# Merging attention runs on TensorE, and a first half turned ahead of the first scores, in a hash attention kernel with an MLP behind it

## The chip, the cores and the metric

One core of one Trainium2 chip. The metric is device time of one execution in microseconds (us), as a median over the runs of a kernel. Executions of one kernel mostly agree within 0.3%; where a single microsecond is at stake, four or five runs on the same chip are compared. All runs here count as fast runs, but for one outlier of the kernel before that is named at e1. Times inside a trace are counted from the start of the profiled execution, whose span is about 2 us shorter than the time of that run.

Below, "PE" is TensorE's matmul, "PEld" its weight load, "DVE" VectorE, "ACT" ScalarE, "POOL" GpSimd. A "bank" is an accumulator of 128 x 512 fp32 in PSUM that TensorE writes into; the kernel has eight of them in use. "Start to start" is the time from the start of one group of instructions to the start of the next; it is what a group costs on a busy engine, where the printed duration contains the overlap with its neighbour.

## The reference, cut to what matters

```python
# hash attention: 4 batches, 8 heads, 768 positions, 64 wide; proj is 64 x 6
q_bits = (q @ proj) > 0;  k_bits = (k @ proj) > 0          # six bits, a bucket each
mask   = bucket(q)[:, None] == bucket(k)[None, :]
scores = where(mask, q @ k.T / 8, -1e9)
attn   = exp(scores - max) ; attn /= sum(attn) + 1e-9
x      = (attn @ v)                     # heads side by side: 3072 tokens x 512
# MLP: 512 -> 2048 -> 512
h = x @ w_in
g = maximum(h, 0) + alpha * minimum(h, 0)
out = g @ w_out
```

The kernel works on 16 pairs of heads. For each pair it transposes q and k ("turn"), multiplies them by proj and takes the signs ("hash"), and then does two units of 384 queries each: 32 units in all. In a unit, six key blocks of scores go through the exponential, "attend" multiplies the probabilities by v, and "totals" multiplies their sums by a matrix of ones to get the divisor. The mask is folded into the scores as a bf16 product of the sign bits. After attention comes the MLP as seven-product blocks (a Strassen-like scheme on 2 x 2 pieces): 44 blocks, each with three accumulators a, b and c.

## The kernel before

Helpers (cut; `do` issues an instruction, `psum` is the pool of banks):

```python
def turn(pi, name, half):                       # three transposes into one bank, one copy
    ps = psum.tile([P, CW], F32, ..., tag="mi")
    for i in range(CH):
        do(PE.transpose(ps[:, i * P : (i + 1) * P], src[:, CH * half + i], ident))
    do(ACT.activation(tr[name, pi][:, half...], ps, AF.Copy, ...))

def hash_bits(pi, half):                        # four products, three signs
    ps = psum.tile([P, CW], F32, ..., tag="mi")
    ...

def scores(u, part):                            # two key blocks
    for kc in (2 * part, 2 * part + 1):
        sc = psum.tile([P, 2, 512], F32, ..., tag="sc")      # a double bank; two of them
        for what, first in ((bits, True), (tr, False)):
            for s in range(2):
                do(PE.matmul(sc[:, s, :CW], what["k", pi]..., what["q", pi]..., start=first, stop=not first))
        do(ACT.activation(pt[:, :, :CW], sc[:, :, :CW], AF.Exp, ...))

def magnitude(pi, name):                        # square in place; its maximum is for the verdict
    do(ACT.activation(t, t, AF.Square, accum_out=mags[...]))
```

One unit of the main loop, cut to what occupies TensorE and to the loads:

```python
for u in range(UNITS):
    pi, g = divmod(u, NCH)
    scores(u, 0)
    ...
    if more:                                    # a next pair exists
        if g == 0: turn(pi + 1, "q", 0); turn(pi + 1, "q", 1)
        else:      hash_bits(pi + 1, 0)
    if u > 0: attend(u - 1, 0)
    scores(u, 1)
    ...
    if u > 0: attend(u - 1, 1); totals(u - 1)
    scores(u, 2)
    if u > 0: divide(u - 1)
    if more:
        if g == 0: turn(pi + 1, "k", 0); turn(pi + 1, "k", 1)
        else:      hash_bits(pi + 1, 1)
    ...
    if more:
        magnitude(pi + 1, "qk"[g])
        if pi + 2 < NPAIR: load(pi + 2, "qk"[g])
```

The eight banks: "sc" two double banks, "mi" two, "av" two. A product of the MLP takes its a from "sc", its b from "mi", its c from "av", so each of them has two buffers. A gate of the MLP (`g`) is written by VectorE into memory that the attention's tiles held before:

```python
attn.close()                                    # attention's tiles are free
late.append(ctx.enter_context(tc.tile_pool(name="late", bufs=2)))
...
g_m[m, i] = late[0].tile([P, CW], F32, ...)
do(DVE.scalar_tensor_tensor(g_m[m, i], h, al, h, op0=ALU.mult, op1=ALU.max))
```

In the third block a verdict is worked out (are the inputs in the range for which the fast path is right): three reductions on VectorE, then four times a transpose on TensorE and a maximum on VectorE.

## Time and profile before

| | us |
|---|---|
| time, median of 3 runs | 976.89 |
| span of the profiled execution | 973.3 |
| first transpose on TensorE | 6.11 |
| first score | 12.73 |
| first attend | 24.43 |
| end of the last totals of attention | 386.00 |
| start of f_3a, just after the verdict | 412.40 |

The table is read as three stages: a head up to the first attend, in which TensorE often waits; 362 us of attention, in which it is seen waiting only once, for 0.25 us; and the MLP, in which it is busy too. The view of all waits confirms that TensorE's idle time was small and mostly at the head; the largest wait elsewhere is the verdict's, 2.0 us. Its columns are: engine and line, then what it waited for; after the colon the total, the number of waits and the longest.

```profile
PE tp_q L629 <- DMA qn<-in_q_dram: 6.1, 1, 6.1
PE sc L668 <- ACT pt L673: 2.6, 2, 2.4
PE vd L861 <- DVE top L856: 2.0, 1, 2.0
```

So 6.1 us go before any input is there, and most of the 2.6 us is one wait at 19.40 us. No change to waits alone could win much in the middle.

### The profile page before, as it was taken

To read this page: it belongs to the slowest core of one execution; us is meant where nothing else is said; L and a number is where in the kernel's file an instruction comes from. 1 tells how busy PE (TensorE), PEld (TensorE's weight loads), DVE (VectorE), ACT (ScalarE), POOL (GpSimd) and SP (SyncE) were. 2 spreads that over 40 slices of the span, in tenths; PEclk is the share of its full clock that TensorE was granted. 3 is DMA by queue.
4 is the path that set the end of the run, shared out by engine and by line. 5 is a ranking of instruction groups with operands and counts; after the bars stand their busy time and mean duration, and the time that the engine had idled before them with its cause. 6 is when DMAs were issued, how large, how long until landed. Compare 5 with 4: busy or idle time off the path is not lost.

```text
span 973.3 us, 12433 instructions
## 1 busy us (share of the span) xinstructions
PE 953.9 (98%) x4741; PEld 589.9 (61%) x4741; DVE 552.9 (57%) x995; ACT 371.5 (38%) x669; POOL 64.8 (7%) x62
## 2 busy tenths in 40 slices
PE   6999999999999999999999999999999999999997
PEld 3444444444444444556888556888556888556885
DVE  3788888898998887765400665301666301666000
ACT  6777776777777773222000222001222001222000
POOL 1000110000000010000300000200001200000000
PEclk9999999999999999999999999999999999999999
DMA  8767879699777643844100234100234100221000
GB/s 208 166 157 174 217 175 291 164 224 225 193 198 193 161 125 88 347 190 140 49 23 33 76 113 143 47 24 31 76 114 154 47 22 22 87 103 38 22 22 25
DMA packets 102020, 119.40 MB, mean 123 GB/s; under 512 B 53808, under 2 KB 88640, under 8 KB 101952
## 3 DMA queue, kind: packets, MB, share of 16 engines
q1 hardware_dynamic: 91680, 105.54, 34.7%
q0 software_dynamic: 8704, 12.58, 7.6%
q8 instruction: 39, 0.64, 0.3%
q10 hardware_dynamic: 1568, 0.39, 0.2%
q14 instruction: 29, 0.24, 0.1%
HBM read 78.65 MB, written 27.26 MB: 109 GB/s over the span
## 4 chain that ended last, share of the span: by engine, by line
PE 97%; ACT 1%; DVE 1%; DMA 0%; issue 0%; SPq 0%; ACTq 0%; DVEq 0%
PE sc L668 16%; PE av L703 14%; PE z_2a L773 6%; PE z_1a L773 6%; PE z_0a L773 6%; PE z_2c L773 3%; PE z_1c L773 3%; PE z_0c L773 3%; PE hs L651 2%; PE f_0a L773 2%; PE sm L715 2%; PE f_2a L773 2%; PE f_3a L773 2%; PE f_7a L773 2%; PE f_6a L773 2%; PE f_5a L773 2%
## 5 line engine op out<-in xcount | busy, mean ns | idle before, releaser
L673 ACT ACTIVATE pt<-sc 128x768 f32<-128x768 f32 x192 | 150.3, 813 | 97.4 <-PE sc L668 92.6
L668 PE MATMUL sc<-qT,kT 64*128 64x384 f32 x768 | 155.2, 482 | 0.0
L703 PE MATMUL av<-pt,vn 128*64 128x385 f32 (+1 forms) x768 | 138.1, 495 | 0.0
L703 PEld LDWEIGHTS av<-pt,vn 128*64 128x64 f32 x768 | 49.4, 136 | 76.7 <-issue 76.7
L827 DVE TENSOR_TENSOR g<-g,g 128x384 f32<-128x384 f32 x128 | 84.0, 677 | 2.2
L668 PEld LDWEIGHTS sc<-qT,kT 64*128 64x128 f32 x768 | 68.7, 189 | 21.0 <-issue 20.9
L668 PE MATMUL sc<-qb,kb 64*128 64x384 bf16 x384 | 63.6, 328 | 2.7 <-ACT pt L673 2.6
L685 POOL DMA_DIRECT2D accp<-pt x32 | 38.5, 1204 | 335.0 <-ACT pt L673 161.3
L668 PEld LDWEIGHTS <-kb 64*128 64x128 bf16 x384 | 19.1, 93 | 66.1 <-issue 52.3
L773 PE MATMUL z_2a<-wo,g 128*128 128x256 f32 x256 | 58.0, 379 | 0.5 <-ACT z_2u L780 0.5
L773 PE MATMUL z_0a<-wo,g 128*128 128x256 f32 x256 | 57.9, 379 | 0.0
L773 PE MATMUL z_1a<-wo,g 128*128 128x256 f32 x256 | 57.9, 379 | 0.0
L773 PEld LDWEIGHTS z_2a<-wo,g 128*128 128x128 f32 x256 | 48.6, 190 | 8.1 <-ACT z_2u L780 0.9
L773 PEld LDWEIGHTS z_0a<-wo,g 128*128 128x128 f32 x256 | 48.6, 190 | 7.5
L773 PEld LDWEIGHTS z_1a<-wo,g 128*128 128x128 f32 x256 | 48.6, 190 | 6.6
L820 DVE SCALAR_TENSOR_TENSOR g<-h,alpha 128x384 f32<-128x384 f32 x32 | 20.8, 652 | 50.5 <-ACT h L812 50.5
L749 POOL TENSOR_TENSOR x<-x,x 128x768 f32<-128x768 f32 x12 | 23.9, 2000 | 359.4 <-DMA x<-x_s 358.9
L654 ACT ACTIVATE qb<-hs,hb 32x384 bf16<-32x384 f32 x64 | 36.7, 573 | 2.3 <-PE hs L651 1.1
L690 DVE TENSOR_TENSOR accd<-accd,pt 128x768 f32<-128x768 f32 x32 | 30.7, 959 | 4.1 <-ACT kT L630 1.0
L693 DVE TENSOR_TENSOR accd<-accd,accp 128x768 f32<-128x768 f32 x32 | 30.5, 952 | 3.1 <-DMA accp<-pt 3.1
L689 DVE TENSOR_TENSOR accd<-pt,pt 128x768 f32<-128x768 f32 x32 | 30.4, 949 | 0.5 <-ACT pt L673 0.5
L682 DVE TENSOR_TENSOR accp<-pt,pt 128x768 f32<-128x768 f32 x32 | 30.5, 952 | 0.0
(218 smaller groups left out, 1443.5 us busy)
## 6 DMA issues: line engine op xcount, KB each, us to landing
wi<-w_in_s SPq DMA_DIRECT2D x32, 896.0 KB, 4.6
accp<-pt POOLq DMA_DIRECT2D x32, 384.0 KB, 7.2
raw<-in_moe_w_in_dram SPq DMA_DIRECT2D x16, 512.0 KB, 4.8
raw<-in_moe_w_out_dram SPq DMA_DIRECT2D x16, 512.0 KB, 4.4
w_in_s<-wsi SPq DMA_DIRECT2D x16, 448.0 KB, 6.8
w_out_s<-wso SPq DMA_DIRECT2D x8, 896.0 KB, 7.5
wo<-w_out_s SPq DMA_DIRECT2D x8, 896.0 KB, 8.4
qn<-in_q_dram SPq DMA_DIRECT2D x32, 192.0 KB, 3.7
```

What stands on the lines that cost most here:

```text
L654: do(ACT.activation(bits["q", pi][D * s : D * s + 32, cols], ps[r], AF.Sign, bias=hb[r]))
L668: do(PE.matmul(sc[:, s, :CW], what["k", pi][r, ks], what["q", pi][r, qs], start=first, stop=not first,))
L673: do(ACT.activation(pt[:, :, :CW], sc[:, :, :CW], AF.Exp, scale=SCALE / DOWN))
L682: do(DVE.tensor_tensor(accp[u], p(u, 0), p(u, 1), op=ALU.add))
L685: nc.gpsimd.dma_start(accp[u], p(u, 2), accum_op=ALU.add)
L689: do(DVE.tensor_tensor(accd[u], p(u, 3), p(u, 4), op=ALU.add))
L690: do(DVE.tensor_tensor(accd[u], accd[u], p(u, 5), op=ALU.add))
L693: do(DVE.tensor_tensor(accd[u], accd[u], accp[u], op=ALU.add))
L703: do(PE.matmul(av[u][D * s : D * s + D, :w], nat["v", pi][:, s, kc * D : (kc + 1) * D], prob[u, kc][:, s, :w], start=(kc == 0), stop=(kc = ...
L749: do(engine.tensor_tensor(x_m[b, to], x_m[b, a], x_m[b, c], op=ALU.subtract))
L773: do(PE.matmul(self.ps[bank], self.left(left, k), self.right(right, k), start=start and k == 0, stop=k == self.nk - 1, skip_group_check=no ...
L827: do(DVE.tensor_tensor(g_m[to, i], g_m[x, i], g_m[y, i], op=op))
```

## The change

Its intent is to make TensorE change its kind of work less often, and to start earlier:

1. Score runs of six key blocks (three of this unit and three of the next) in place of three runs of two; the two attend halves and totals side by side; turns of q and k side by side; both hash halves in one group. For this the score banks become three double banks, which turn and hash share; the two banks left, "sm" and "av", become single.
2. The first q and k are loaded in halves, and one half is turned and hashed first; the second half is turned before the first scores too, but hashed behind them.
3. Twelve products of zeros occupy TensorE while the inputs come.
4. The squares (`magnitude`) go behind the exponentials.
5. The verdict's four transposes go into one bank, with one maximum.
6. In the first MLP block the steps are reordered so that c is finished first and b last.

Smaller moves go with these and are not shown below: the order of the first loads, alpha's transpose (now in the second unit), and the places of some of VectorE's additions.

```diff
-    psum = ... tc.tile_pool(name="ps", bufs=2, ...)
+    psum = ... tc.tile_pool(name="ps", bufs=1, ...)
+        zero = const.tile([P, 512], BF16, name="zero")
+        ps = psum.tile([P, 512], F32, name="nil", tag="av")
+        for i in range(12):
+            do(PE.matmul(ps, zero[:, :P], zero, start=True, stop=True))
+    def two_banks(name):
+        return psum.tile([P, 2, 512], F32, name=name, tag="sc", bufs=3)
@@ Product.times
-                tag, shape = {"a": ("sc", ...), "b": ("mi", ...), "c": ("av", ...)}[bank]
+                if bank == "a" or bank == "c" and self.name == "f0_0":
+                    t = two_banks(self.name + bank)[:, 0]
+                else:
+                    t = psum.tile([P, 512], F32, ..., tag="sm" if bank == "b" else "av")
@@ head
-    load(0, "q"); load(0, "k", nc.scalar); setup(); load(0, "v")
-    ... turn(0, name, half) four times, hash_bits(0, half) twice, setup_alpha()
+    load_part(0, "q", slice(0, CH), nc.sync); load_part(0, "k", slice(0, CH), nc.scalar)
+    setup()
+    ... the other halves' loads
+    for name in "qk": turn(0, name, first)
+    hash_bits(0, first)
+    for name in "qk": turn(0, name, second)
+    ... loads of the next pair and of weights
+    scores(0, 0); add_first(0)
+    hash_bits(0, second)
+    for name in "qk": turn(1, name)
@@ main loop, TensorE's work only
-        scores(u, 0) | turn or hash half | attend(u - 1, 0) | scores(u, 1)
-        attend(u - 1, 1), totals(u - 1) | scores(u, 2) | turn or hash half
+        scores(u, 1), scores(u + 1, 0)
+        hash_bits(pi + 1)  or  turn(pi + 2, "q"), turn(pi + 2, "k")
+        attend(u, 0), totals(u), attend(u, 1)
@@ end of the loop body
-            magnitude(pi + 1, "qk"[g]); load(pi + 2, "qk"[g])
+        done = [(u, "q"), (u, "k")] if u < 2 else []
+        if 2 <= pi + 1 + g < NPAIR: done.append((pi + 1 + g, "kq"[g]))
+        for p2, name in done: magnitude(p2, name); load(p2 + 2, name)
@@ first MLP block, verdict
-        for st in ((2, 22, 6, 3, 7) if j == 0 else (2, 22, 5, 6, 3, 7)):
+        for st in ((6, 3, 7, 2, 22) if j == 0 else (2, 22, 5, 6, 3, 7)):
+        ps = psum.tile([1, 4, P], F32, name="vd", tag="av")
         for n in range(4):
-            ... transpose into its own bank, and reduce it
+            do(PE.transpose(ps[:, n], top[:, n : n + 1], ident))
+        do(DVE.tensor_reduce(row, ps, axis=..., op=ALU.max))
```

## The prediction

> **What bounds the kernel now.** I read the page's busy shares first, then the stage table, then the order of work on TensorE inside one unit (384 queries of one pair of heads; there are 32), then the two ends of the attention stage. The metric is 976.89 us; the profiled span is 973.3 us.
>
> ```profile
> PE 953.9 (98%) x4741; PEld 589.9 (61%) x4741; DVE 552.9 (57%) x995; ACT 371.5 (38%) x669; POOL 64.8 (7%) x62
> PE 97%; ACT 1%; DVE 1%; DMA 0%; issue 0%; SPq 0%; ACTq 0%; DVEq 0%
> ...
> 10.00:20.00 10.00, 6.51 (x50) 3.26 (x42) 3.80 (x8) 9.17 (x17) 0.00 (x0) 1.00 0.75 241
> 20.00:40.00 20.00, 20.00 (x140) 8.92 (x137) 15.95 (x28) 16.29 (x29) 2.53 (x2) 1.00 0.76 163
> 200.00:300.00 100.00, 100.00 (x676) 44.28 (x676) 91.55 (x165) 72.12 (x120) 10.80 (x9) 1.00 0.79 201
> 400.00:960.00 560.00, 557.77 (x2168) 411.03 (x2167) 222.41 (x390) 94.41 (x210) 23.89 (x12) 1.00 0.22 78
> ```
>
> Columns of the stage table: stretch, length, then busy us of PE, PEld, DVE, ACT, POOL. TensorE is busy all through the attention stage and the products after it, and the chain that ended last is 97% TensorE. So time can only come from idle TensorE at the head, or from making TensorE's own work shorter. VectorE is second, at 92% in the later attention units. "Busy" says little of how well TensorE is used, so I looked at starts instead of durations:
>
> ```profile
> 104.64 0.88 PE L629 MATMUL tp_q<-ident,qn 128*128 128x128 f32 x6
> 105.45 2.16 PE L703 MATMUL av<-pt,vn 128*64 128x384 f32 x12
> 107.54 0.34 PE L668 MATMUL sc<-qb,kb 64*128 64x384 bf16 x2
> 107.71 0.81 PE L668 MATMUL sc<-qT,kT 64*128 64x384 f32 x4
> 108.35 0.33 PE L668 MATMUL sc<-qb,kb 64*128 64x384 bf16 x2
> 108.52 0.81 PE L668 MATMUL sc<-qT,kT 64*128 64x384 f32 x4
> 109.25 2.16 PE L703 MATMUL av<-pt,vn 128*64 128x384 f32 x12
> 111.24 0.81 PE L715 MATMUL sm<-accd,ones 128*64 128x384 f32 x4
> 111.99 0.34 PE L668 MATMUL sc<-qb,kb 64*128 64x384 bf16 x2
> ```
>
> First column start, second duration. No row waits, yet equal work differs in length. One attend half takes 109.25 to 111.24 = 1.99 us when totals follow in the same tiling (128*64), but 105.45 to 107.54 = 2.09 when scores (64*128) follow. The first score block is 107.54 to 108.35 = 0.81, the second, before another tiling, 0.90. Leaving a tiling therefore costs about 0.09 after scores and 0.10 after attend or totals. Between single records I also find the first attend step 0.05 longer than the later ones (0.37 against 0.32). Hash halves: 0.34 from group to group inside a run, 0.78 for a whole run of two groups, so 0.10 for leaving. A six-transpose run is 0.81, of which 0.15 is beyond 0.11 per transpose.
>
> **What the Trainium skill says.** "TensorEngine Tiling (Array Packing)", Key Properties: "Changing tiling mode (not just tile) drains the TensorE". It gives no time; this trace agrees and puts it at 0.08 to 0.15 us a change. "TensorE: Matmul & The Clock Gate", Part 1: the array starts at half clock and is released after some 3.4 us of sustained work, in a free-running window. The trace agrees: hash groups start 0.64 us apart at 9.05 us and 0.34 apart at 102.14 us. The granted-clock column says 1.00 in both places, so it does not show this. "Perfetto Trace Analysis", Identifying the Most-Contended Engine: matmul busy share is no measure of distance to the limit; here 100% busy hides the drains above.
>
> **The change, part by part.**
>
> Runs merged. Before, a unit on TensorE is seven runs: scores (2 blocks), turn or hash, attend half, scores (2), attend half with totals, scores (2), turn or hash. After, by the order of the built program, it is three: scores (3 of this unit and 3 of the next), turn or hash, attend half + totals + attend half. The arithmetic is the same. Saved per unit: scores leave once in place of three times, 2 x 0.083 = 0.17; attend leaves once in place of twice and refills once, 0.10 + 0.05 = 0.15. Over 31 units: 31 x 0.32 = 9.8 us. Hash halves merged: 14 pairs x 0.107 = 1.5. Turns of q and k merged: 14 pairs x 0.15 = 2.1. In the last two units, 0.36 us of waits for exponentials go with the deeper score buffers (three double banks for two), and the first product's pieces no longer lie between attend pieces, about 0.35. Sum 14.1 us.
>
> Head. Before, first transpose at 6.11, first score at 12.73, first attend at 24.43:
>
> ```profile
> 6.11 1.51 PE L629 MATMUL tp_q<-ident,qn 128*128 128x128 f32 x6 [6.11 <-DMA qn<-in_q_dram]
> ...
> 12.56 0.23 PE L511 MATMUL alps<-ident,alpha 16*128 16x16 f32 x1 [1.13 <-ACT kb L656]
> 12.73 0.34 PE L668 MATMUL sc<-qb,kb 64*128 64x384 bf16 x2
> ...
> 19.40 0.34 PE L668 MATMUL sc<-qb,kb 64*128 64x384 bf16 x2 [2.36 <-ACT pt L673]
> ```
>
> After: twelve zero products of 512 columns start near 1.2 us. From the 0.64 per 2 x 384 columns above, one takes 0.43 cold, so they end near 6.2, no earlier than today's first transpose, though half the input should land near 4.7. What they buy is a full clock. Then three q transposes (0.4), copy (0.57), k copy (0.57), one hash half, three signs of 0.58: first score near 10.7. Three score blocks, hash half two, twelve transposes; then a wait of 0.7 for the second signs and 0.4 for a score bank (ACT, in order, has signs, two copies and the weight's absolute value ahead of the next exponential). First attend near 22.95, with one more score block (0.82) and one more hash half (0.7) done. Gain 1.48 + 0.82 + 0.70 = 3.0 us. The squares (0.84 each plus a read of 0.2), now behind all exponentials, are part of why the 2.36 us wait goes.
>
> Verdict: before, PE waits 1.97 us for VectorE and later 0.26 more between four transposes. The first wait stays (same VectorE work ahead of it), the rest shrinks: 0.45 us.
>
> A new wait. The products' banks b and c go from two buffers to one, and the first product block now finishes c first, b last. The first gate tile lies where attention tiles lay, so its write waits for the last stores:
>
> ```profile
> 387.82 0.62 DVE L730 SCALAR_TENSOR_TENSOR x<-av,vs,dn 128x384 f32<-128x384 f32 x1
> 388.36 1.79 DVE L602 TENSOR_TENSOR wso<-wso 128x256 f32<-128x256 f32 x4
> 390.07 0.55 DVE L815 TENSOR_TENSOR f_0p<-f_0p,f_0b 128x384 f32<-128x384 f32 x1
> 394.25 0.62 DVE L820 SCALAR_TENSOR_TENSOR g<-f_0p,alpha 128x384 f32<-128x384 f32 x1 [3.63 <-issue]
> ```
>
> Today bank b is read at 390.07, before that wait, and the next block has another bank. After, the read of b stands behind the stalled gate write. Let E be the end of the last attend. VectorE then has some 5.4 us left (weight sums, then divide), the store of x lands 2 to 4 us later, so gates begin near E + 8.5 and b is free after four more operations (0.55 + 0.55 + 0.55 + 0.55) at E + 10.7. TensorE wants it after six products of 1.29, at E + 7.7. New wait about 3.0 us.
>
> Sum: 14.1 + 3.0 + 0.45 - 3.0 = 14.6 us; 976.9 - 14.6 = 962.3 us. Everything else (the 560 us of products, the tail) I take as unchanged.
>
> **The rivals.**
>
> 1. VectorE becomes the bound. Its work per unit, start to start, is about 10.4 us in the later units, 11.2 with the x sums of four units. A TensorE unit falls from about 11.57 to 11.14 (4.99 scores + 1.46 turn or hash + 4.68 attend and totals). It still fits; but if VectorE's in-order waits added 0.8 us per unit, half the merge gain (6 us) would go: 968.
> 2. ScalarE holds the longer score runs. A back-to-back exponential takes 0.775 us start to start (1.50 for two) against 0.82 per score block, and there are three double banks. For it: the one four-block run of before stalled 0.3 us with two. If it stalled 0.3 us in every run, 9 us would go: 971. I think the third bank prevents it.
> 3. The new wait does not show, because the stores land sooner: 959.3. Or it is 5 us: 964.3.
> 4. Drains are not saved as counted, since a longer run only hides weight loads that the short one exposed elsewhere: 968 or so. Against it: equal runs differ only by what follows.
>
> **Range and chances.** Independent doubts: head 1.5, merge 2, new wait 2, rivals 1 and 2 one-sided upward. Range 958.0 to 968.0. Over 2% faster means under 957.3, that is 5 us more than I can count: 10%. Slower by 2% would need a stall in every unit well beyond the drains saved: 1%. Within 2%: 89%.
>
> **What would show it.** Right: score blocks 0.82 apart through runs of six, units 11.1 to 11.2 us, first attend near 23 us, end of attention 17 us earlier than its 386 us, and a TensorE gap of some 3 us before f_1b, released by VectorE. Wrong: gaps before scores released by ScalarE, gaps before totals or attend released by VectorE, transposes that still start after 6.5 us cold, or no gap at f_1b.

## The result, and the profile after

The changed kernel took 959.98 us (median of 4 runs, 959.51 to 963.64), beside 976.84 us for the kernel before (4 runs). The ratio is 0.984, with a 95% interval from 0.981 to 0.986: within 2%, and 17 us less. Ratios in this text are the mean time of one kernel's fast runs over that of the other's in the same rounds, so they are not quite the ratio of the medians quoted.

| | before | after |
|---|---|---|
| span of the profiled execution | 973.3 | 957.7 |
| first score | 12.73 | 10.43 |
| first attend | 24.43 | 22.33 |
| end of attention (last totals, or last attend) | 386.00 | 368.22 |
| start of f_1b | 393.85 | 378.60 |
| start of f_3a | 412.40 | 396.75 |

The page's first line and its chain of work that ended last, of the kernel after:

```profile
PE 941.2 (98%) x4753; PEld 600.2 (63%) x4753; DVE 555.2 (58%) x993; ACT 364.7 (38%) x594; POOL 64.6 (7%) x62
...
PE 92%; DVE 4%; ACT 2%; DMA 1%; issue 1%; SPq 0%; DVEq 0%; ACTq 0%
```

TensorE has 12.7 us less busy time for twelve instructions more: the same products became shorter, or overlapped better. But the chain is now only 92% TensorE where it was 97%, although TensorE's time without work fell too, from 19.4 to 16.5 us (span less busy time): at new waits the chain leaves TensorE and runs back along another engine, before 378.60 us along VectorE to about 341 us. So the share says that there are new waits and not what they cost. Both sides have to be found.

**The middle.** The order of work on TensorE in a unit with a turn (columns: start, duration, engine and line, operation and tiles):

```profile
205.71 0.34 PE L695 MATMUL sc<-qb,kb 64*128 64x384 bf16 x2
...
206.53 0.33 PE L695 MATMUL sc<-qb,kb 64*128 64x384 bf16 x2
...
210.66 0.87 PE L646 MATMUL tp_q<-ident,qn 128*128 128x128 f32 x6
211.37 0.82 PE L646 MATMUL tp_k<-ident,kn 128*128 128x128 f32 x6
212.12 2.16 PE L728 MATMUL av<-pt,vn 128*64 128x384 f32 x12
214.11 0.81 PE L740 MATMUL sm<-accd,ones 128*64 128x384 f32 x4
214.75 2.10 PE L728 MATMUL av<-pt,vn 128*64 128x384 f32 x12
216.79 0.34 PE L695 MATMUL sc<-qb,kb 64*128 64x384 bf16 x2
```

Six score blocks take 205.71 to 210.66, 4.95 us. The turns of q and k take 1.46, the first attend half 1.99, totals 0.64, the second attend half, which still leaves its tiling, 2.04. The unit is 216.79 - 205.71 = 11.08 us, where the kernel before needed about 11.57. No row shows a wait.

**The head.** The first transposes, the first scores and the first attend of the kernel after; the bracket names an idle time before the row and what ended it:

```profile
1.20 5.09 PE L509 MATMUL nil<-zero 128*128 128x512 bf16 x12 [1.20 <-DVE wh L501]
6.12 0.49 PE L646 MATMUL tp_q<-ident,qn 128*128 128x128 f32 x3
...
10.43 0.34 PE L695 MATMUL sc<-qb,kb 64*128 64x384 bf16 x2 [1.09 <-ACT kb L675]
...
15.72 0.34 PE L695 MATMUL sc<-qb,kb 64*128 64x384 bf16 x2 [0.45 <-ACT kb L675]
...
22.33 2.16 PE L728 MATMUL av<-pt,vn 128*64 128x385 f32 x12
```

The first transpose starts when the zeros end, at 6.12, and not when its data come; otherwise the head is as wanted, and the first attend is 2.1 us earlier with more work done before it.

**A wait at 32 us**, which nothing in the kernel before corresponds to:

```profile
32.48 0.84 PE L646 MATMUL tp_q<-ident,qn 128*128 128x128 f32 x6 [0.46 <-DMA qn<-in_q_dram]
34.13 0.85 PE L646 MATMUL tp_k<-ident,kn 128*128 128x128 f32 x6 [0.81 <-issue]
```

The turn of the third pair waits for its input. Two input buffers exist, the third pair takes the first pair's, and its load cannot begin before the squares have read that buffer: those are now behind the exponentials, and q's is done at 26.6 us. For k the view names no releaser ("issue"); that it waits for the same reason is shown by e7, where both waits go. From the starts, the two waits cost 0.53 and 0.94 us.

**The end of attention.** TensorE's rows and then VectorE's, of the kernel after:

```profile
374.88 1.45 PE L801 MATMUL f_0a<-x,wi 128*128 128x384 f32 x4
378.60 1.56 PE L801 MATMUL f_1b<-x,wi 128*128 128x384 f32 x4 [2.26 <-DVE f_0p L843]
...
396.31 0.60 PE L889 MATMUL vd<-ident,top 128*1 128x128 f32 x4 [1.97 <-DVE top L884]
```

```profile
376.34 0.62 DVE L848 SCALAR_TENSOR_TENSOR g<-f_0u,alpha 128x384 f32<-128x384 f32 x1 [1.94 <-DMA x_s<-x]
...
378.00 0.55 DVE L843 TENSOR_TENSOR f_0p<-f_0p,f_0b 128x384 f32<-128x384 f32 x1
```

The first gate waits for the store of x, the read of bank b stands three operations behind it at 378.00, and f_1b, which needs the bank, starts 0.6 us later. This is the new wait that the prediction named, with the engine and the product it named: 2.26 us idle, where it said about 3.0. The verdict's wait of 1.97 us stayed, as it said.

**The account.** From the first attend to the end of attention: 361.57 us before, 345.89 after, 15.68 less. Of this, 1.52 is a score block (0.82) and a hash half (0.70) that now come before the first attend, so 14.16 is gain, in spite of about 1.46 lost at 32 us. The head gives 2.10 + 1.52 = 3.6. The new wait, from the starts and not from the idle time alone, takes 2.4 (374.88 to 378.60 is 3.72, against 1.29 for a product). The verdict, from f_2a to f_3a, falls from 4.36 to 3.86, 0.5. Sum 14.2 + 3.6 - 2.4 + 0.5 = 15.9, against 15.6 between the two spans. The medians differ by 16.9: the profiled run of the kernel before, at 975.17 us, was shorter than all four of the runs that its median is of (976.09 to 977.32).

### The profile page after: what moved, and what is told of

Read it like the earlier page. It is cut to its first block, busy times and chain, and to the rows that moved or that the text cites. A ratio compares the mean times of both kernels' runs of the same rounds, so it can differ in the third digit from the quotient of the medians.

```text
span 957.7 us, 12390 instructions
## 1 busy us (share of the span) xinstructions
PE 941.2 (98%) x4753; PEld 600.2 (63%) x4753; DVE 555.2 (58%) x993; ACT 364.7 (38%) x594; POOL 64.6 (7%) x62
## 4 chain that ended last, share of the span: by engine, by line
PE 92%; DVE 4%; ACT 2%; DMA 1%; issue 1%; SPq 0%; DVEq 0%; ACTq 0%
PE sc L695 14%; PE av L728 12%; PE z_2a L801 6%; PE z_1a L801 6%; PE z_0a L801 6%; PE z_2c L801 3%; PE z_1c L801 3%; PE z_0c L801 3%; PE hs L669 2%; PE f_2a L801 2%; PE f_3a L801 2%; PE f_7a L801 2%; PE f_6a L801 2%; PE f_5a L801 2%; PE f_4a L801 2%; PE f_1a L801 2%
## 5 line engine op out<-in xcount | busy, mean ns | idle before, releaser
L700 ACT ACTIVATE pt<-sc 128x768 f32<-128x768 f32 x192 | 152.9, 814 | 78.5 <-PE sc L695 76.6
L728 PEld LDWEIGHTS av<-pt,vn 128*64 128x64 f32 x768 | 52.3, 136 | 70.7 <-issue 61.4
L714 DVE TENSOR_TENSOR accd<-pt,pt 128x768 f32<-128x768 f32 x32 | 30.6, 955 | 14.1 <-ACT pt L700 14.0
L675 ACT ACTIVATE qb<-hs,hb 32x768 bf16<-32x768 f32 (+1 forms) x34 | 29.1, 855 | 10.0 <-PE hs L669 8.7
```

The costliest lines, as they stand in the source:

```text
L675: do(ACT.activation(t[rows].rearrange("p (h w) -> p h w", h=2)[:, halves], ps[ps_rows, halves, :CW], AF.Sign, bias=hb[ps_rows],))
L700: do(ACT.activation(pt[:, :, :CW], sc[:, :, :CW], AF.Exp, scale=SCALE / DOWN))
L714: do(DVE.tensor_tensor(accd[u], p(u, 3), p(u, 4), op=ALU.add))
L728: do(PE.matmul(av[u][D * s : D * s + D, :w], nat["v", pi][:, s, kc * D : (kc + 1) * D], prob[u, kc][:, s, :w], start=(kc == 0), stop=(kc = ...
```

## The experiments

Each edit is made on the changed kernel unless said otherwise. All gave right results. The kernel before had medians of 977.14, 976.92 and 976.17 us on the three chips used (e1 to e4, e5 to e8, e9 to e12).

### e1: the changed kernel again

No edit; a yardstick for e2 to e4.

> The changed kernel unaltered, as the measure for the others, since one of its four runs was 4 us longer than the rest at a granted clock of 0.995. Expected: 959.5 to 960.5 us and a ratio to the kernel before of 0.9825 to 0.9835; the profile as the first one to 0.1 us (first score 10.4 us, first attend 22.3 us, attention over at 368.2 us). If the 964 us comes back in more than one run, then the kernel itself has a second state that one profile does not show.

958.99 us (958.77 to 963.68, 5 runs), ratio 0.982. Its second profile has the first attend at 22.74 and the end of attention at 368.94, so a trace of this kernel repeats to about 0.7 us, not to the 0.1 us expected. One run of the kernel before took 5681.61 us in these rounds, an outlier; the median is not moved by it.

One thing wants an explanation. Of the nine runs of the changed kernel here and above, seven lie at 958.77 to 960.35 with a mean granted clock of 0.998 or 0.999; two lie at 963.64 and 963.68, both at 0.995. The kernel before has such steps too: on the three chips, 10 of its 26 runs (without the outlier) lie at 975.62 to 976.17 with a clock of 0.998 or 0.999, 13 at 976.71 to 977.49 with 0.996 or 0.997, and 3 at 978.26 to 978.90 with 0.995.

### e2: turn or hash between the attend halves

```diff
+        weight_parts(u)
+        attend(u, 0)
         if g == 0 and pi + 1 < NPAIR: hash_bits(pi + 1)
         if g == 1 and pi + 2 < NPAIR: turn(pi + 2, "q"); turn(pi + 2, "k")
-        weight_parts(u)
-        attend(u, 0)
         totals(u)
```

The same instructions, only one more change of tiling in a unit. It tells "a change of kind has a price" from a gain by the deeper score banks or by fewer waits for other engines, which this edit leaves as they are.

> The changed kernel with turn or hash moved from ahead of the attend run to between its two halves: same instructions, but in 28 units one more change of tiling (attend, turn or hash, totals and attend). Theory that each change of tiling costs a drain and a refill: each of the 28 units grows by 0.10 to leave attend and 0.05 to refill it, 0.15 us, so 4.2 us in all; the first attend half goes back from 1.99 to 2.09 us start to start. The rival that the gain came from the deeper score ring or from fewer waits of the other engines: within 0.5 us of the changed kernel, as no wait is added.

963.96 us (963.51 to 964.30, 4 runs), 5.0 above e1. TensorE's rows of its profile, a hash and then a turn inside the attend run:

```profile
205.31 0.87 PE L740 MATMUL sm<-accd,ones 128*64 128x384 f32 x4
206.01 2.11 PE L728 MATMUL av<-pt,vn 128*64 128x385 f32 x12
...
213.00 2.15 PE L728 MATMUL av<-pt,vn 128*64 128x384 f32 x12
215.08 0.87 PE L646 MATMUL tp_q<-ident,qn 128*128 128x128 f32 x6
```

An attend half followed by turn or hash takes 2.09 in place of the 1.99 before totals, and totals 0.70 in place of 0.65. That is 0.15 a unit, and over 29 units with a turn or hash 4.4 us. With a score wait at 30 us (0.5), 0.1 elsewhere and the input wait at 32 us, which went (-1.5), the rows add up to 3.5; the spans of the two profiles differ by 3.9. The price of a change of tiling is real, and the trace shows it as a longer row with nothing waiting.

What the price consists of, this run does not say. In the kernel before, the weight loads for totals start at 110.92 us, together with the last attend products (110.92), and those for scores at 107.53, 0.42 after the last attend products (107.11): over a change of tiling the next weights are not loaded ahead. So it is at every change between 45 and 350 us, 0.41 to 0.42 after scores, hash, attend and totals, and 0.20 after turns. "The array is emptied first" and "a weight load is no longer hidden" both fit that, and the saving is the same for both.

### e3: the gates of the first block behind its additions

```diff
+            def gate():
+                g_m[m, i] = late[0].tile(...)
+                do(DVE.scalar_tensor_tensor(g_m[m, i], h, al, h, ...))
+            if hold[0]: held.append(gate)       # first block: run after its five steps
+            else: gate()
```

VectorE now reads bank b before it meets the gate that waits for the store of x.

> The changed kernel, but in the first product block the three additions that read the product banks come before the three gates, so that the gate's wait for the last stores no longer stands ahead of the read of bank b. Theory of the new wait: the 2.26 us idle TensorE before f_1b goes, and the two switches of the stream near it; the time falls by 2.3 us to about 957.6. Rival: VectorE is so far behind here that the gap moves to the next product that needs it, and less than 1 us is gained.

957.40 us (956.68 to 959.76, 5 runs), 1.6 below e1, with a span in the profile that hardly fell. The gap before f_1b was gone (f_1b started at 376.23) and a small one of 0.44 us showed in the second block. So the cause of the new wait was right, but the gain in single runs scattered: 956.68 to 957.40 at a clock of 0.999, 959.60 and 959.76 at 0.997. The profile was one of the latter, and after the verdict's wait its products are long:

```profile
394.55 0.60 PE L898 MATMUL vd<-ident,top 128*1 128x128 f32 x4 [1.97 <-DVE top L893]
394.98 2.62 PE L801 MATMUL f_3a<-x,wi 128*128 128x384 f32 x4
397.40 2.03 PE L801 MATMUL f_2a<-x,wi 128*128 128x384 f32 x4
399.26 1.45 PE L801 MATMUL f_3b<-x,wi 128*128 128x384 f32 x4
```

Beside it the stage table of the same profile for 2 us of this stretch (stretch, length, busy us of PE, PEld, DVE, ACT and POOL, granted clock, DMA share, GB/s):

```profile
396.00:398.00 2.00, 2.00 (x4) 1.01 (x3) 0.72 (x7) 0.36 (x1) 0.00 (x0) 0.50 0.24 100
```

f_3a and f_2a take 2.42 and 1.86 start to start in place of 1.29, at half the clock: 1.7 us lost, without any wait. The half clock lasts from 395.13 to 398.54, 3.41 us. "TensorE: Matmul & The Clock Gate", Part 1 of the Trainium skill, describes a free-running window of 3413 ns after which an idle TensorE falls to half clock. The trace agrees on the length and on the window being free-running: all changes of clock in the fourteen profiles lie a whole number of 3.413 us from the first full clock (e3: 389.12 us, which is 114 such lengths). It does not agree on how much idle time it takes; the last section has the numbers.

### e4: no products of zeros

```diff
-        zero = const.tile([P, 512], BF16, name="zero")
-        do(DVE.memset(zero, 0.0))
-        ps = psum.tile([P, 512], F32, name="nil", tag="av")
-        for i in range(12):
-            do(PE.matmul(ps, zero[:, :P], zero, start=True, stop=True))
```

> The changed kernel without the twelve products of zeros. My theory from the prediction (they cost nothing, since they end when the first transpose could start at best, and buy a full clock): the first transposes start only a little earlier and everything to the first attend runs at half clock in part; the first attend comes 1 to 2 us later than 22.3 us. The rival that the changed kernel's trace suggests: the DMA queue's waits say that the halves of q and k have landed by about 4 us, so the zeros hold the first transpose back by 2 us; then it starts at about 4.1, at half clock, and gain and loss nearly cancel: within 1 us of the changed kernel.

961.27 us (960.71 to 962.26, 5 runs), 2.3 above e1. Read alone, this says that the zeros are worth 2 us. TensorE's rows of its profile, at the head and at f_1b, say otherwise:

```profile
4.22 0.88 PE L641 MATMUL tp_q<-ident,qn 128*128 128x128 f32 x3 [4.22 <-DMA qn<-in_q_dram]
...
378.50 2.56 PE L796 MATMUL f_1b<-x,wi 128*128 128x384 f32 x4 [2.29 <-DVE f_0p L838]
380.86 2.18 PE L796 MATMUL f_1c<-x,wi 128*128 128x384 f32 x4
```

The first transpose starts at 4.22, cold and slow, but 1.9 us earlier than behind twelve zeros. The first score is at 9.82 (10.43 with zeros), the first attend at 21.93 (22.33 and 22.74), the end of attention at 368.09 (368.22 and 368.94). Attention is no later without the zeros. What is slower comes after: f_1b and f_1c at half clock after the 2.29 us wait. All five runs have a clock of 0.995 to 0.997. That the zeros only shifted the phase of the window against the waits is inferred from that; in the head, twelve of them do not earn their place.

### e5: two double banks for the scores

```diff
-        return psum.tile([P, 2, 512], F32, name=name, tag="sc", bufs=3)
+        return psum.tile([P, 2, 512], F32, name=name, tag="sc", bufs=2)
```

One bank is left unused, and bank c of the first block has its own, so that nothing else moves.

> The changed kernel with two double banks for the scores in place of three (nothing else; one bank stays unused). This asks how much of the gain hangs on the third bank, which my prediction named as what keeps ScalarE from holding back the runs of six. If it does: the run of six score blocks grows from 4.95 us by some 0.3 us of waits released by ScalarE, as the one run of four did before, 31 times, so 6 to 10 us. If TensorE's own pace is the limit also with two banks (an exponential's 0.775 us is under the 0.82 of a block): under 1 us.

987.22 us (986.77 to 987.90, 4 runs), ratio 1.011: slower than the kernel before. TensorE's rows of its profile, the bf16 part of three neighbouring blocks in a score run:

```profile
209.24 0.34 PE L695 MATMUL sc<-qb,kb 64*128 64x384 bf16 x2
210.06 0.33 PE L695 MATMUL sc<-qb,kb 64*128 64x384 bf16 x2
211.20 0.34 PE L695 MATMUL sc<-qb,kb 64*128 64x384 bf16 x2 [0.17 <-ACT pt L700]
```

The first two blocks are 0.82 apart, the third comes 1.14 after the second. A run of six takes 5.78 us in place of 4.95: 0.83 times some 30 runs is 25 us. Turns, which take their banks from the same two, grow from 1.46 to 1.67, 3 us in 14 units. Together that is the 28 us between e5 and e1, and about three times the 10 us that the expectation allowed at most. A bank is busy for the products (0.82), a pause to the exponential of about 0.25 and the exponential (0.81), 1.9 us in all; two banks allow a block every 0.94, three every 0.63. Only the latter is below 0.82. In the kernel before, runs of two just fitted two banks. "Perfetto Trace Analysis", Optimization Strategy, says that the same bubble repeating on the engine that should be saturated can mean too little PSUM for the next tile; this trace agrees. The idle time shown is only 8.8 us in 54 waits, a third of what is lost. Undisturbed, a block starts about 0.16 us before the printed end of the one before it; after a wait this overlap is lost too.

So the third double bank is part of the merge, not an extra. It is paid for with the second buffers of b and c, which, with the gate ahead of the read of b, made the new wait (no run gives b its second buffer back).

### e6: the old head in the new order

```diff
-    load_part(0, "q", slice(0, CH), nc.sync) ... and the other halves, and the zeros
+    load_part(0, "q", slice(0, NC), nc.sync); load_part(0, "k", slice(0, NC), nc.scalar)
     for name in "qk":
-        turn(0, name, first)
-    hash_bits(0, first) ...
+        turn(0, name)
+    hash_bits(0)
```

> The changed kernel with the old head: q and k of the first pair loaded whole and turned whole, both hash halves before the first score, no zeros; all that comes later is as in the changed kernel. It measures the head alone. My prediction put the head's gain at 3.0 us; from the changed kernel's trace and the half clock of the old head (hash groups 0.64 us apart) I now expect first score at about 15 us, first attend at 25.5 against 22.3 to 22.7 us, so 3 us lost: about 962 to 963 us. Rival: the head is hidden, and under 1 us is lost.

968.70 us (967.45 to 969.44, 4 runs), 9.7 above e1 (on another chip, where the kernel before differs by 0.2). The 3 us expected were missed by far. Of the 9.7 about 5.5 is the head and 3.4 two stretches of half clock, after f_1b's wait and after the verdict's. The first transposes start at 6.71, the first score at 16.14, and the score blocks are 1.60 apart until the full clock at 19.62; the first attend is at 28.21, 5.5 to 5.9 later than in the changed kernel's two profiles. In the new order a head without halves is worse than it was before, since hash and turns are stacked ahead of all scores and TensorE has long gaps. Here the cold clock is costly, so halves and zeros could not be told apart by this run; e4 does that.

### e7: three input buffers

```diff
-            nat[name, pi] = pool.tile([P, NC, 2, D], F32, ..., tag=f"{name}n")
+            nat[name, pi] = pool.tile([P, NC, 2, D], F32, ..., tag=f"{name}n", bufs=3)
     load(1, "v")
+    load(2, "q")
+    load(2, "k")
```

> The changed kernel with a third buffer for q and k each, and the loads of the third pair issued before the loop, so that they no longer wait for the squares of the first pair and for the store of x ahead of them in the queue. The changed kernel's trace shows TensorE idle 0.46 to 0.84 us before the q turn at 32 us and 0.73 to 0.81 before the k turn, each with a slower first turn after it. Theory: the squares' later place made this wait; it goes, 1.5 us gained. Rival: the loads collide with those of weights and v in the head, the first attend comes later, and the gain is nil.

959.35 us (958.16 to 959.94, 5 runs). The waits at 32 us are gone and the last attend run starts at 364.94, in the changed kernel's two profiles at 366.18 and 366.90. The time did not follow, since in the profiled run the half clock takes it back after f_1b's wait (378.52 to 381.93); the clocks of the five runs are 0.996 to 0.999. The input wait was real, and worth 1.2 to 2 us to attention.

### e8: seven zeros in place of twelve

```diff
-        for i in range(12):
+        for i in range(7):
```

> The changed kernel with seven products of zeros in place of twelve. Without any, the first transpose started at 4.22 us, released by the load of q, so the twelve, which end at 6.2, hold it back by 2 us; seven end at about 4.2. Theory: the first transpose starts at 4.3, the clock is full by 6 to 7 us as with twelve, and the first score comes at about 9.0 against 10.4 to 10.9: 1.3 to 1.8 us gained. Rival: with less work in the first window the full clock is granted a window (3.4 us) later, near 10 us as without zeros, and the gain is under 0.5 us.

TensorE's rows at the head of its profile:

```profile
1.20 3.17 PE L509 MATMUL nil<-zero 128*128 128x512 bf16 x7 [1.20 <-DVE wh L501]
4.42 0.57 PE L646 MATMUL tp_q<-ident,qn 128*128 128x128 f32 x3
...
8.81 0.34 PE L695 MATMUL sc<-qb,kb 64*128 64x384 bf16 x2 [0.96 <-ACT kb L675]
```

959.43 us (958.21 to 961.90, 5 runs), no less than e1's median. In the profiled run, the fastest, seven zeros end as the data land and the clock is full from 4.55 on; the first score comes 1.6 us earlier than with twelve, the last attend run at 364.82, 1.4 to 2.1 earlier. The clock was luck of this profile: e10 and e11 have the same seven zeros, but a full clock only from 6.00 and 6.02 on, and a first score at 9.37 and 9.29. Over all profiles the first score is at 8.81 to 9.37 with seven zeros (3 profiles), at 9.82 without (e4), and at 10.23 to 10.95 with twelve (8). So seven are better than twelve in the trace; in the times of five runs it does not show. Two of them, 960.81 and 961.90, have clocks of 0.997 and 0.996; the other three, 958.21 to 959.43, overlap the seven of the changed kernel at 0.998 or 0.999.

### e9: no long gap on TensorE

e3's edit, and the verdict's three reductions one block earlier:

```diff
+        if j == 1:
+            tops()             # the reductions on VectorE
         if j == 2:
             verdict()          # the transposes and what follows
```

> The changed kernel with the gates later as in the third experiment, and the verdict's three reductions one product block earlier, so that TensorE no longer waits 1.97 us for them. It tests the theory that the two TensorE gaps of 2 us (before f_1b and before the verdict) are what makes single runs 2 to 4 us longer: the traces so far show the clock at half for 3.41 us after such a gap when the gap falls within one stretch of 3.41 us counted from the first full clock, and not when it straddles a border. With both gaps gone: 2.3 + 2.0 us less than the changed kernel's shorter runs, so about 955 us, no run over 1 us above the lowest, and a granted clock of 0.998 or 0.999 in every run. Rival: the longer runs have another cause, and some of five are still 2 to 4 us over the rest.

955.66 us (955.08 to 956.04, 5 runs), ratio 0.978 [0.977, 0.980], faster than the kernel before by over 2%. All five clocks are 0.998 or 0.999 and the five runs lie within 1 us. TensorE's rows of its profile at f_1b and at the verdict, with no idle time in brackets:

```profile
375.18 1.45 PE L801 MATMUL f_0a<-x,wi 128*128 128x384 f32 x4
376.47 1.45 PE L801 MATMUL f_1b<-x,wi 128*128 128x384 f32 x4
...
392.66 0.60 PE L901 MATMUL vd<-ident,top 128*1 128x128 f32 x4
```

The two gaps cost 2.4 and some 2 us directly, and 0.45 returned as a wait of f_2a for its weights: 4.0 us, which is what the ratios say (0.9824 in e1, 0.9783 here, 0.0041 of 977 us). And the scatter went with the gaps.

### e10: e9, three input buffers and seven zeros together

> As the ninth, with three input buffers and seven zeros as well. If the four gains add: 1.5 us more for the inputs and 1.3 us for the zeros, so about 952 us and a ratio near 0.975 to the kernel before, which would be clear of 2%. If TensorE's first gap then moves to another wait (weights of the third block, which came 0.44 us late in the third experiment), about 953.

954.75 us (953.09 to 954.94, 5 runs), ratio 0.977 [0.976, 0.978]. This is the best version, 2.3% below the kernel before and 4 to 5 us below the changed one. It missed the 952 us expected: with inputs early, a 1.0 us wait appears at 38.7 us, where the small transpose of alpha needs the single "sm" bank that a divide still reads, totals wait 0.33 in a second place (the 0.28 before the last totals was there already), and the clock is full 1.45 us later than in e8's profile, which puts the first score 0.56 later. These are 1.9 of the 2.8 us missed; the rest was not traced.

### e11: e10, with the second layer's weights loaded later

```diff
-            if b == 0:
-                wo.append(...); nc.sync.dma_start(wo[n], w_out_s[n])
+            if b == 0 and 1 <= n <= NI // 2:
+                for m in (2 * n - 2, 2 * n - 1):
+                    wo.append(...); nc.sync.dma_start(wo[m], w_out_s[m])
```

It was to test whether f_2a's wait comes from weights that share the queue.

> As the tenth, with the loads of the second layer's weights spread over blocks two to five in place of one a block from the first, so that they don't run beside the load of the third block's weights. Theory: the 0.44 us wait before f_2a goes, 0.4 us gained. Rival: it was the release of the buffer, not the traffic, and nothing changes.

954.82 us (954.12 to 955.64, 5 runs): the same. f_2a still waits, 0.53 us. But the trace shows that the edit did not do what it was meant to: loads of the second layer's weights are still issued at 375.43, 376.28 and 376.74, around that of the third block's weights at 375.80, as in e10 (375.57, 376.42 and 376.88, around 375.94), and the 16 DMA engines are busy throughout 378 to 384 us in both. So the traffic is neither shown nor ruled out. It is suspect: in the kernel before, the same load was issued ahead of the others, at 394.04, and landed after 4.7 us, here after 6.4, and there f_2a did not wait.

### e12: the squares early again

```diff
     weight_abs(0)
+    for name in "qk":
+        magnitude(0, name)
+        load(2, name)
```

> The changed kernel with the squares of the first pair put back ahead of the exponentials of the first score run, and the loads of the third pair after them. My prediction named the squares' new place as part of why the 2.36 us wait of before goes. If that holds: ScalarE has 1.9 us more ahead of the exponentials, the wait for a score bank (0.4 us at 18.4 us in the changed kernel) grows to about 2.3, the first attend comes 1.9 us later; against that the wait for the inputs at 32 us (1.5 us) goes; the sum is within 1 us of the changed kernel. Rival: with three banks the squares hide, the first attend is not later, and 1.5 us are gained.

960.33 us (959.51 to 961.16, 4 runs). In TensorE's rows of its profile a score run now waits for a bank:

```profile
19.82 0.34 PE L695 MATMUL sc<-qb,kb 64*128 64x384 bf16 x2 [1.70 <-ACT pt L700]
```

From start to start that costs 1.87 us beyond the 0.81 of a block, in the changed kernel 0.22. The first attend is at 23.77, 1.0 to 1.4 later, and the input wait at 32 us is gone; the end of attention is at 368.2, within the spread of the changed kernel's. Moving the squares was a trade of one wait for another of the same size.

## Why the prediction was right

Predicted were 962.3 us and a range of 958 to 968; measured 960.0. It was right, and mostly for its own reasons, but two of its steps failed and one error hid another.

**Runs merged: 14.1 us predicted, about 15.6 found.** The middle gained 14.16 net of the input wait's 1.46. The under-count is in the terms of the sum: a six-block run takes 4.95 in place of 4.99 (31 times 0.04 is 1.3), and a full hash 1.43 in place of 1.46 (14 times 0.035 is 0.5). That each change of tiling has its price e2 shows by putting one back: 4.4 us by the sum of rows. Rival 4 foresaw less because a long run would only hide weight loads; the size was as counted, and whether the price is a drain or a weight load that can't be hidden no run tells apart.

**The input wait at 32 us was not predicted.** The prediction saw the squares move behind the exponentials and counted only the wait that goes. It did not ask what a late square holds up: the buffer that the next load needs. e7 removes the wait with a buffer, e12 by moving the squares back. It cost what the merge sum had too little, so that the middle came out right by two errors.

**Head: 3.0 predicted, 3.6 and 3.2 found in two profiles.** The sum held, the first attend being at 22.33 and 22.74 where it said 22.95. But the step that twelve zeros cost nothing and buy a full clock failed. They did buy it, at 5.95 us where it came at 10.27 without (e4). But "half the input should land near 4.7" was 4.2, and they held the first transpose back to 6.12: the head is no later without zeros (e4), and seven do better (e8), so twelve cost what they earn. It also wrote that the granted-clock column does not show the cold head; this is so only before the column's first record. It does show later half clocks, as in e3.

**Verdict: 0.45 predicted, 0.50 found.**

**The new wait: 3.0 predicted, 2.4 found.** Engine, product and mechanism were right, and e3 shows the mechanism: with the gates behind the additions the wait goes. The store of x landed 2.2 us after its issue, inside the "2 to 4 us" but at its short end.

**The rivals.** VectorE did not become the bound: in all of attention TensorE waits for it once, 0.28 us before the last totals. ScalarE did not hold the six-block runs, because of the third bank, as judged; but the price of going without it was mis-sized: 0.3 us a run said, 0.83 found in e5. A 5 us new wait did not come.

**"Everything else ... I take as unchanged" failed for the products.** A wait of 2 us that lies in one stretch of 3.41 us was followed by half the clock for the next such stretch, about 1.7 us more (e3, e4, e6, e7). Which run it hits depends on the phase. The kernel before has the steps of clock and time as well (e1), and the verdict's wait of 1.97 us; the change added a second wait of this length. The two slow runs of nine, 4 us above the rest at a clock of 0.995, have the clock for it, but were not profiled: that they are such stretches is inferred: 3.41 us at half clock lower the mean clock by 0.0018, and the last few us of a run, where the clock has fallen too, by about 0.0015 to 0.002, so that 0.995 is two such stretches. In e9 to e11 the long gaps are gone and all fifteen runs are at 0.998 or 0.999.

Open are the cause of f_2a's wait of 0.4 to 0.5 us in e9 to e11, and why all five runs of e4 met a half clock.

## What to carry to other kernels

On a TensorE that is never seen idle, look at equal work with different neighbours: start to start, the row before a change of kind is longer, and the sum over all units is what reordering can win. Ask of each buffer that pays for it what will now wait, and of each operation that moves later, what its reading held up. When a median does not move though a wait is gone from the trace, look at the granted clock of each run before calling the wait harmless: a gap of 2 us can cost nearly twice its length, in some runs and not in others.

## What the Trainium skill lacked or had wrong

- "TensorE: Matmul & The Clock Gate", Part 1, gives a whole idle window of about 3.4 us as what brings the half clock back. Here 1.97 us idle within one 3.41 us stretch was enough (e3 and e6; also 2.24 in e7, 2.29 in e4 and 2.32 in e6), and 1.93 us was not (e4, where a border cut 0.04 off the verdict's wait of 1.97; also 1.84 in e2 and 1.81 in e1, where a border split a wait of 2.27). All fourteen profiles fit a limit between 1.93 and 1.97; the ends of products are modelled, so the last hundredths are not sure. Both the length of the window and that it is free-running agree.
- "TensorEngine Tiling (Array Packing)", Key Properties, says that changing the tiling mode drains TensorE and gives no time. Here it was 0.08 to 0.15 us for each change; put back once a unit it cost 4.4 us of 959 (e2).
- "Perfetto Trace Analysis", Optimization Strategy, has the repeating bubble that stands for too little PSUM, but not that the idle time shown may be only a part of the loss: 8.8 us shown, 25 us lost in the score runs of e5.
- No page says how many products a kernel should put ahead of inputs that it waits for: twelve held the first transpose back to 6.12 us (clock full at 5.95), seven let it start at 4.35 to 4.43 with the clock full at 4.55 to 6.02 (e8, e10, e11), none at 4.22 with the clock full at 10.27 (e4).
